# Seven block products for eight in gate, up and the queries of a transformer layer, with fp32r sums on 64-row halves and queries passed through DRAM

## The chip, the cores and the metric

One core of a Trainium2 chip. The metric is device time in microseconds (us), the median of several executions.

## The reference, cut to what matters

```python
# x [2048, 448]; wq [448, 16*256]; wo [16*256, 448]; w_gate, w_up [448, 1792]; w_down [1792, 448]; all bf16
xn = layernorm(x)
q  = (xn @ wq)                                  # 16 heads of 256
k, v = last 512 rows of the caches, 8 heads, each for two query heads
s  = softmax(q @ k.T / 16) @ v @ wo             # attention branch
g  = silu((gelu(xn @ w_gate) * (xn @ w_up)) @ w_down)
return x + s * g
```

The four chunks of 512 tokens are numbered 0 to 3. A "head" below is one of the 64 pairs of head and chunk.

## The kernel before: the parts that matter

Every instruction is recorded by a helper and put into the engine's program with its semaphore waits, so all products of one helper carry one line number (L328). Gate, up and query products have 448 rows to contract: three times 128, and 64 that are left. They are made as products of 64 rows, two at a time on the two halves of the array, each half writing another PSUM bank; halfway through, the halves change banks:

```python
def group(units, lo, hi, start, stop, phases=(0, 1)):
    for p in phases:                                  # phase 1: the halves change banks
        ...
        for (b, w, wr, cols, reads, rreads, xts) in units:
            for k in ks:
                for u, j in ((0, ph), (1, 1 - ph)):   # u: half of the array, j: bank
                    rows = slice(R * u, R * u + R)    # R = 64
                    l = wr[rows] if k == NK else w(j, k)[rows]
                    lst.append((bank[b + j][:, lo:hi], l, xnT[rows, k, cols], ...))
            before = [last_row[b][0]] if ... last_row[b][1] != ph else []   # wait for the other half
```

Queries are made just before they are used, in groups of 8 or 12 heads between the heads of attention, and stay in SBUF. For one head, attention multiplies scores, takes the exponential on ScalarE, the normalisation on VectorE, transposes by DMA (SBUF to SBUF), and multiplies by the values two heads later:

```python
for m in range(NS):                                   # NS = 64
    if m in groups:                                   # 0, 8, 20, 32, 44, 56
        for i in range(m, groups[groups.index(m) + 1], 2):
            q_group(i, ...)                           # all products of two query heads
    s_mm(m)                                           # 8 products; Exp; tensor_scalar; two dma_t of 128 KB
    ...
    if len(late) == LAG:                              # LAG = 2
        pv(late.pop(0))                               # 8 products, wait for the transposes of head m - 2
```

The softmax here doesn't subtract the row's maximum and nothing guards it: scores larger than these inputs give would overflow.

Of the kernel before, what the change touches and what calls it, by code (L numbers as in the profile page):

```python
# [8 lines left out]
F32 = mybir.dt.float32  # L9

LN_EPS = 1e-5
P = 128
# [3 lines left out]
class Buf:  # L16
# [3 lines left out]
    __slots__ = ("lo", "hi", "writer", "readers")  # L20

    def __init__(self, lo, hi):
        self.lo, self.hi = lo, hi
        self.writer = None
        self.readers = []

# [10 lines left out]
class Plan:  # L37
# [16 lines left out]
    def buf(self, lo=0, size=0):  # L54
        b = Buf(lo, lo + size)
        self.bufs.append(b)
        return b

    def reuse(self, new):


        for b in new:
            for x in self.bufs:
                if x not in new and x.lo < b.hi and b.lo < x.hi:
                    b.readers.extend(x.readers)
                    if x.writer is not None:
                        b.readers.append(x.writer)

    def op(self, eng, fn, reads=(), writes=(), dma=False, after=()):
        o = Op(eng, fn, dma)  # L70
        raw = {b.writer: None for b in reads if b.writer is not None}
        deps = dict(raw)
        for b in writes:
            if b.writer is not None:
                deps[b.writer] = None
            deps.update((x, None) for x in b.readers)


        for d in deps:
            if d.eng == eng and not d.dma and not dma and (eng == "pe" or d not in raw):  # L80
                continue
            o.deps.append(d)
        o.deps.extend(after)
        for b in writes:
            b.writer, b.readers = o, []
        for b in reads:
            b.readers.append(o)
        self.ops.append(o)
        return o
# [75 lines left out]
def bass_recurrent_scan__sliding_block_cached__geglu_ffn__prompt_kernel(  # L165
# [32 lines left out]
    HG = 8  # L198
    NG = Hq // HG
    QS = 12  # L200

    es = ExitStack()
    with es:
# [3 lines left out]
        def place(name, shape, dt, at=None):  # L207
            size = {BF16: 2, F32: 4}[dt]
# [40 lines left out]
        kT, a, _ = place("kT", [P, Hkv, 2, W], BF16)  # L249
        b_kT = sbuf_bufs(a, 2 * W * 2, Hkv)  # L250
        va, a, _ = place("va", [P, Hkv, NJ, Dh], BF16)
        b_va = [K.buf() for g in range(Hkv)]
        wq, a, _ = place("wq", [P, NK, HD], BF16)
        wqr, a, _ = place("wqr", [P, Hq, P], BF16)
        b_wql = [[K.buf() for i in range(3)] for g in range(NG)]
# [8 lines left out]
        rw = base[0]  # L264
        wo, _, rw_end = place("wo", [P, NCO, D], BF16)
        b_wo = sbuf_bufs(rw, 8 * D * 2, NCO // 8)
        x4, a, a2 = place("x4", [P, NT, D], BF16, at=rw)
        b_x4 = sbuf_bufs(a, D * 2, NT)
        NXN = (rw_end - a2) // (DP * 2)
        xn, a, a2 = place("xn", [P, NXN, DP], BF16, at=a2)  # L270
        b_xn = [[K.buf(a + i * DP * 2, D * 2), K.buf(a + i * DP * 2 + D * 2, R * 2)] for i in range(NXN)]
        assert a2 <= rw_end

        rf = base[0]
        wgu, a, at = place("wgu", [P, 2, NK, F], BF16, at=rf)
        wgur, _, at = place("wgur", [P, F], BF16, at=at)
        b_wgu = K.buf(a, at - a)
        FBL = [0, 3, 6, 9, NF]
        b_wl = [[K.buf() for j in range(2)] for i in range(4)]
        b_wlr = [[K.buf() for j in range(2)] for i in range(3)]  # L280
        wd, a, at = place("wd", [P, NF, D], BF16, at=at)
        b_wd = K.buf(a, at - a)
        actT, a, at = place("actT", [P, 2, NF, QC], BF16, at=at)
        b_actT = [sbuf_bufs(a + i * NF * QC * 2, QC * 2, NF) for i in range(2)]
        NGL = 3
        gl, a, at = place("gl", [P, NGL, QC], BF16, at=at)
        b_gl = sbuf_bufs(a, QC * 2, NGL)


        NPT, NPN, NP32 = 3, 3, 3  # L290
        pT, a, at = place("pT", [P, NPT, 2, 2, NJ, P], BF16, at=rf)
        b_pT = [sbuf_bufs(a + i * QC * NJ * 2, QC * NJ, 2) for i in range(NPT)]
        pn, a, at = place("pn", [P, NPN, 2, W], BF16, at=at)
        b_pn = sbuf_bufs(a, 2 * W * 2, NPN)
        p32, a, at = place("p32", [P, NP32, W], F32, at=at)
        b_p32 = sbuf_bufs(a, W * 4, NP32)
        assert at <= b_wgu.hi
        oT, a, at = place("oT", [P, NCO, QC], BF16, at=b_wgu.hi)
        b_oT = sbuf_bufs(a, QC * 2, NCO)
        qT, a, at = place("qT", [P, QS, 2, QC], BF16, at=b_gl[0].lo - (QS - HG) * 2 * QC * 2)  # L300
        assert b_oT[-1].hi <= a
        b_qT = [[K.buf(a + (h * 2 + e) * QC * 2, QC * 2) for e in range(2)] for h in range(QS)]

# [7 lines left out]
        def qs(n):  # L311
            return QS - 1 - n % QS

# [7 lines left out]
        def act(o, i, func, reads, writes, scale=1.0):  # L321
            K.op("act", lambda e, o=o, i=i: e.activation(o, i, func, scale=scale), reads, writes)  # L322
# [167 lines left out]
        def gu_evac(n, b):  # L490
            c, f = divmod(n, NF)
            s = n % NGL
            act(gl[:, s, :], bank[b], ACT.Gelu_apprx_tanh, (b_ps[b],), (b_gl[s],))
            K.op("dve", lambda e: e.tensor_tensor(actT[:, c % 2, f, :], bank[b + 1], gl[:, s, :], ALU.mult),  # L494
                 (b_ps[b + 1], b_gl[s]), (b_actT[c % 2][f],))

        def down(c, pairs):
            for t4 in range(4):
                t = c * 4 + t4
                b = bk(pairs, t4)  # L500
                mms([(bank[b][:, 0:D], actT[:, c % 2, f, t4 * P:(t4 + 1) * P], wd[:, f, :], f == 0, f == NF - 1)
                     for f in range(NF)], [b_wd] + b_actT[c % 2], (b_ps[b],))
# [66 lines left out]
        def load_k(g):  # L569
            dma_t(kT[:, g, :, :], A_k_cache[0, g, Sk - W:Sk, :], (), (b_kT[g],))  # L570

        def load_v(g):
            dma("pool", va[:, g, :, :],
                A_v_cache[0, g, Sk - W:Sk, :].rearrange("(j p) d -> p j d", p=P), (), (b_va[g],))

        def load_wq(g):
            lo, hi = g * HG * Dh, (g + 1) * HG * Dh
            dma("pool", wq[:, :, lo:hi], A_wq[0:K3, lo:hi].rearrange("(k p) f -> p k f", p=P), (), (b_wql[g][0],))
            for e in range(2):
                dma("pool", wqr[R * e:R * e + R, g * HG:(g + 1) * HG, :],  # L580
                    A_wq[K3:D, lo:hi].rearrange("p (h e f) -> p h e f", e=2, f=P)[:, :, e, :], (), (b_wql[g][1 + e],))

        DOWN_AT = {NF + 5: 0, 2 * NF + 1: 1}
# [4 lines left out]
        NU = NQC * NF  # L588
        cur, nxt = (0, 2), (4, 6)
        for n in range(4, NU, 2):  # L590
# [4 lines left out]
            if ln_t[0] < 8 or n >= 12:  # L595
                ln_a()
            cur, nxt = nxt, cur
# [4 lines left out]
            if n == 32:  # L602
                for g in range(NG):
                    load_wq(g)
                for g in range(Hkv):
                    load_v(g)
                for g in range(Hkv):
                    load_k(g)
                K.reuse(b_wo)
                for i in range(NCO // 8):  # L610
                    dma("pool", wo[:, i * 8:(i + 1) * 8, :],
                        A_wo.rearrange("(c p) d -> p c d", p=P)[:, i * 8:(i + 1) * 8, :], (), (b_wo[i],))
                for t in range(NXR):
                    dma("pool", xr[:, t, :], x_view[:, t, :], (), (b_xr[t],))
            if n + 1 in DOWN_AT:
                down(DOWN_AT[n + 1], cur)
                cur, nxt = nxt, cur


        def q_group(n, pairs):  # L620

            c, h = divmod(n, Hq)
            units = [(b, lambda j, k, i=i: wq[:, k, (h + i) * Dh + j * P:(h + i) * Dh + (j + 1) * P],
                      wqr[:, h + i, :], slice(c * QC, (c + 1) * QC), b_wql[h // HG][:1], b_wql[h // HG][1:], b_xnT[c * 4:c * 4 + 4])
                     for i, b in enumerate(pairs)]
            group(units, 0, QC, True, True)
            for i, b in enumerate(pairs):
                s = qs(n + i)
                act(qT[:, s, 0, :], bank[b], ACT.Copy, (b_ps[b],), (b_qT[s][0],))
                K.op("dve", lambda v, s=s, b=b: v.tensor_copy(qT[:, s, 1, :], bank[b + 1]),  # L630
                     (b_ps[b + 1],), (b_qT[s][1],))
# [3 lines left out]
        def s_mm(m):  # L635
            s, g = qs(m), m % Hq // 2
            for t4 in range(4):
                b = AB[t4]
                mms([(bank[b], qT[:, s, e, t4 * P:(t4 + 1) * P], kT[:, g, e, :], e == 0, e == 1) for e in range(2)],
                    [b_kT[g]] + b_qT[s], (b_ps[b],))  # L640
# [51 lines left out]
        NS = NQC * Hq  # L692
        groups = [0, HG] + list(range(HG + QS, NS, QS)) + [NS]

        act(tmp[:, 1, 0:1], nhalf[:, :], ACT.Exp, (b_nhalf,), (b_tmp[1][0],))
        K.reuse([b for y in b_qT[QS - HG:] for b in y])
        AB.extend(bk(cur, j) for j in range(4))
        BB.extend(bk(nxt, j) for j in range(4))
        for m in range(NS):
            if m in groups:  # L700
                for i in range(m, groups[groups.index(m) + 1], 2):
                    q_group(i, (cur, nxt)[i // 2 % 2])
                if m == 0:
                    K.reuse([b for x in b_pT for b in x] + b_pn + b_p32)
            s_mm(m)
            if m < LAG:
                down(NQC - LAG + m, nxt)
                if m == LAG - 1:
# [85 lines left out]
```

## Time and profile before

556.33 us (556.25 to 556.43). How to read the table: a matrix product that runs back to back with its neighbours starts 0.216 us after them (512 columns, 128 rows, or a pair of 64-row products), so a stage's floor can be counted.

| what | number | from |
|---|---|---|
| span of the profiled run | 554.7 us | page |
| TensorE busy | 547.6 us, 99% | engine table |
| TensorE's share of the chain of waits | 98% | chain |
| one head (16 products) | 3.45 us | distance of its first Exp to that of the next |
| first score product | 126.6 us | tile of the keys |

The top of the page of the kernel before: engine, busy us, share of the span, instructions.

```profile
span 554.7 us, 9719 instructions
PE 547.6 (99%) x3603; PEld 261.2 (47%) x3628; DVE 317.2 (57%) x817; ACT 273.6 (49%) x727; POOL 32.7 (6%) x64
```

From its costliest groups (line, engine, operation, written tile <- read tiles, shapes, count, then busy us and mean ns of one, then idle time before):

```profile
L328 PE MATMUL bank<-pT,va 128*128 128x512 bf16 x512 | 120.8, 379 | 0.0
L328 PE MATMUL bank<-xnT,wq 64*128 64x512 bf16 x768 | 94.4, 376 | 0.0
L328 PEld LDWEIGHTS bank<-xnT,wq 64*128 64x128 bf16 x768 | 36.9, 94 | 46.5 <-ACT p L643 2.1
```

TensorE (PE) never idles before a query or a value product, and a weight load (PEld) of 64 rows takes 94 ns, far less than the product over which it hides.

A window of 20 us that holds only heads of attention, kernel before: the second line is start:end, length, busy time of each engine with instructions, granted clock, share of the 16 DMA engines, GB/s.

```profile
core 0: us, PE busy (x) PEld busy (x) DVE busy (x) ACT busy (x) POOL busy (x), PEclk, DMA share, GB/s
368.00:388.00 20.00, 19.89 (x92) 9.09 (x93) 16.67 (x53) 16.83 (x53) 0.00 (x0) 1.00 0.82 158
```

And the tile of the transposed probabilities, kernel before:

```profile
L319 SPq DMA_TRANSPOSE pT<-pn x128: 1231/1261/2443, 129.0 to 524.0; - x128
  DVE pn L647: 5.4, 6
  PEld bank L328: 0.2, 1
DMA to landing us min/median/max: 2.7/2.8/4.6
```

In this tile view the first line gives size and number of the transfers, the indented lines tell who waited for them (us in all, times), and the last one how long they took from issue to landing. The transposes alone fill 0.82 of the DMA engines in this window (0.71 to 0.82 in the windows of heads that were read), and they land in 2.8 us, so that TensorE practically never waits for one.

### The profile page before, as it was taken

The page shows a single profiled execution, that of the slowest core. Times are in us where ns is not written, and L with a number is a line of the kernel's source. Part 1 is how long each engine was busy: PE and PEld are TensorE (multiplying, and loading weights), DVE is VectorE, ACT ScalarE, POOL GpSimd, SP SyncE. Part 2 cuts the span into 40 slices and gives each one's busy share as a digit, 9 for nine tenths or more (in the row PEclk, how much of TensorE's full clock was granted, in tenths as well). Part 3 has the DMA queues.
Part 4 walks back from the last instruction along what each step waited for, and adds up shares of the span by engine and source line. Part 5 has one row for each costly group of instructions (what it writes and reads, how often), then busy time and mean ns, then how long its engine had stood idle before and what let it go on. Part 6 is the DMA issues. An engine that isn't in the chain of part 4 may idle for free.

```text
span 554.7 us, 9719 instructions
## 1 busy us (share of the span) xinstructions
PE 547.6 (99%) x3603; PEld 261.2 (47%) x3628; DVE 317.2 (57%) x817; ACT 273.6 (49%) x727; POOL 32.7 (6%) x64
## 2 busy tenths in 40 slices
PE   8999999999999999999999999999999999999997
PEld 5554444444544444554444444544444454444455
DVE  6673734443385588326588745258747625858722
ACT  5432324353485588205588635058747505758600
POOL 1120580000000000000000000000000000000000
PEclk9999999999999999999999999999999999999999
DMA  9540399901156077413086803157704713618601
GB/s 295 115 141 9 79 302 307 213 1 39 38 134 96 5 149 157 88 35 92 1 153 152 153 1 77 33 94 164 146 11 95 134 34 90 153 19 153 153 8 34
DMA packets 163599, 57.63 MB, mean 104 GB/s; under 512 B 151456, under 2 KB 160672, under 8 KB 163552
## 3 DMA queue, kind: packets, MB, share of 16 engines
q1 hardware_dynamic: 159488, 45.16, 38.8%
q0 software_dynamic: 3296, 11.27, 6.7%
q8 instruction: 29, 0.48, 0.4%
q10 hardware_dynamic: 768, 0.57, 0.3%
q14 instruction: 18, 0.15, 0.1%
HBM read 17.92 MB, written 1.84 MB: 36 GB/s over the span
## 4 chain that ended last, share of the span: by engine, by line
PE 98%; DMA 1%; issue 0%; DVE 0%; SPq 0%; ACT 0%
PE bank L328 98%; DMA x<-in_A_x_dram 1%; SPq L316 0%; DVE stats L375 0%; ACT xnT L322 0%; DVE tmp L681 0%; ACT ve L391 0%; DVE ofin L684 0%; PE bank L426 0%; DVE mv L378 0%
## 5 line engine op out<-in xcount | busy, mean ns | idle before, releaser
L643 ACT ACTIVATE p<-bank 128x512 f32<-128x512 f32 x256 | 149.2, 597 | 103.3 <-PE bank L328 101.4
L647 DVE TENSOR_SCALAR pn<-p,rden 128x512 bf16<-128x512 f32 x256 | 124.6, 487 | 14.4 <-DMA pT<-pn 5.4
L328 PE MATMUL bank<-pT,va 128*128 128x512 bf16 x512 | 120.8, 379 | 0.0
L328 PE MATMUL bank<-kT,qT 128*128 128x512 bf16 x487 | 117.8, 379 | 2.0 <-ACT qT L322 1.0
L328 PE MATMUL bank<-wo,oT 128*128 128x448 bf16 (+2 forms) x544 | 97.7, 341 | 0.0
L328 PE MATMUL bank<-xnT,wq 64*128 64x512 bf16 x768 | 94.4, 376 | 0.0
L328 PE MATMUL bank<-xnT,wgu 64*128 64x512 bf16 (+2 forms) x768 | 83.9, 350 | 0.4 <-ACT xnT L322 0.4
L328 PEld LDWEIGHTS bank<-pT,va 128*128 128x128 bf16 x512 | 50.1, 98 | 60.4 <-DMA pT<-pn 0.2
L328 PEld LDWEIGHTS bank<-kT,qT 128*128 128x128 bf16 x512 | 49.6, 98 | 61.3 <-issue 2.5
L328 PEld LDWEIGHTS bank<-wo,oT 128*128 128x128 bf16 x544 | 52.0, 98 | 45.5
L630 DVE CAST qT<-bank 128x512 bf16<-128x512 f32 x64 | 42.9, 692 | 51.9 <-PE bank L328 51.9
L322 ACT ACTIVATE qT<-bank 128x512 bf16<-128x512 f32 x64 | 38.2, 597 | 60.7 <-PE bank L328 59.1
L328 PEld LDWEIGHTS bank<-xnT,wq 64*128 64x128 bf16 x768 | 36.9, 94 | 46.5 <-ACT p L643 2.1
L322 ACT ACTIVATE gl<-bank 128x512 bf16<-128x512 f32 x56 | 33.2, 597 | 49.4 <-PE bank L328 46.2
L494 DVE TENSOR_TENSOR actT<-bank,gl 128x512 bf16<-128x512 f32 x56 | 37.8, 689 | 33.4 <-PE bank L328 26.6
L328 PEld LDWEIGHTS bank<-xnT,wgu 64*128 64x128 bf16 x768 | 36.9, 94 | 37.4 <-issue 0.7
L643 ACT ACTIVATION_READ_ACCUMULATOR p<-bank 128x1 f32 x256 | 52.8, 206 | 0.0
L646 DVE RECIPROCAL rden<-rsum 128x1 f32<-128x1 f32 x256 | 40.4, 158 | 20.6 <-ACT p L643 20.0
L681 DVE SCALAR_TENSOR_TENSOR tmp<-bank,g 128x448 f32<-128x448 f32 (+2 forms) x17 | 10.1, 597 | 72.5 <-PE bank L328 72.5
L666 DVE CAST oT<-bank 128x512 bf16<-128x512 f32 x64 | 43.8, 684 | 6.9 <-PE bank L328 6.9
L328 PE MATMUL bank<-wd,actT 128*128 128x448 bf16 x224 | 43.0, 353 | 0.0
L322 ACT ACTIVATE oT<-bank 128x512 bf16<-128x512 f32 x64 | 39.1, 611 | 7.0 <-PE bank L328 7.0
(39 smaller groups left out, 182.9 us busy)
## 6 DMA issues: line engine op xcount, KB each, us to landing
wo<-in_A_wo_dram POOLq DMA_DIRECT2D x4, 896.0 KB, 19.0
wq<-in_A_wq_dram POOLq DMA_DIRECT2D x2, 1536.0 KB, 10.0
va<-in_A_v_cache_dram POOLq DMA_DIRECT2D x8, 256.0 KB, 13.9
pT<-pn SPq DMA_TRANSPOSE x128, 2.8
xr<-in_A_x_dram POOLq DMA_DIRECT2D x16, 112.0 KB, 2.3
out_dram<-ofin SPq DMA_DIRECT2D x15, 112.0 KB, 1.7
wd<-in_B_w_down_dram SPq DMA_DIRECT2D x1, 1568.0 KB, 7.6
x<-in_A_x_dram SPq DMA_DIRECT2D x2, 448.0 KB, 4.4
```

What stands on the lines that cost most here:

```text
L322: K.op("act", lambda e, o=o, i=i: e.activation(o, i, func, scale=scale), reads, writes)
L328: ins = e.matmul(o, lhsT=l, rhs=r, start=st, stop=sp)
L494: K.op("dve", lambda e: e.tensor_tensor(actT[:, c % 2, f, :], bank[b + 1], gl[:, s, :], ALU.mult), (b_ps[b + 1], b_gl[s]), (b_actT[c % 2][ ...
L630: K.op("dve", lambda v, s=s, b=b: v.tensor_copy(qT[:, s, 1, :], bank[b + 1]), (b_ps[b + 1],), (b_qT[s][1],))
L643: K.op("act", lambda e, b=b, r=r, z=z: e.activation(p32[:, z, :], bank[b], ACT.Exp, scale=att_scale, accum_out=rsum[:, r:r + 1]), (b_ps[b] ...
L646: K.op("dve", lambda e, r=r: e.reciprocal(rden[:, r:r + 1], rsum[:, r:r + 1]), (b_rsum[r],), (b_rden[r],))
L647: K.op("dve", lambda e, r=r, z=z, y=y, t=t4 % 2: e.tensor_scalar(pn[:, y, t, :], p32[:, z, :], rden[:, r:r + 1], None, op0=ALU.mult), (b_p ...
L666: K.op("dve", lambda v, i=i, b=b: v.tensor_copy(oT[:, i, :], bank[b]), (b_ps[b],), (b_oT[i],))
L681: K.op("dve", lambda e: e.scalar_tensor_tensor(out=tmp[:, s, c0:c1], in0=bank[b][:, c0:c1], scalar=0.5, in1=g2[:, t, c0:c1], op0=ALU.mult, ...
```

## The change

The intent: take one slot in fourteen of TensorE away. For two chunks of tokens and two weight blocks (gate and up; or the two 128-column halves of a query head), the 256 x 256 part of the contraction is a 2 x 2 block product. Seven products of sums give it in place of eight (Winograd's form), so 26 products of 64 rows stand for 28. This is done for 46 blocks: 14 of gate and up in chunks 2 and 3, 32 of the queries. The sums are kept in fp32r, a 4-byte type that the TensorE multiplies. Every product is split into two 64-row halves, laid into 13 slots per block by a table of offsets made by hand or search, and a small scheduler that models the engines gives the order. Because a query product now covers two chunks at once, all queries are made ahead of attention, stored to DRAM (64 times 256 KB), and loaded back, 8 heads ahead.

```diff
+        xf1, b_xf1, o = rhs_forms(57 * KB, "xf1")        # sums of activations, F32R
+        wf, a, at = at_(o, "wf", [P, NWF, 7, 2, P], F32R) # sums of weights, made on GpSimd
+        qd = nc.dram_tensor("q_all", [NQC * Hq, P, 2 * QC], BF16)
...
+        GP = 13
+        AT = {'P1l': 2, 'P1h': 0, 'P2l': 9, 'P2h': 11, 'L11a': 7, ..., 'Lda': 39, 'Ldb': 40, 'Ldh': 35}
+        SLOT, PSEM, ESEM = 0.216, 0.40, 0.03      # the scheduler's costs: PSEM + ESEM from half to half
...
+            p1 = mm(at("P1l", "P1h"), A, LH, Wb(B1, 0), X(0, t1), rb(r1), ready, **wt)        # bf16
+            seed = copy_task(..., lambda: bk_(C), lambda: bk_(A), ...)                         # bank to bank, ScalarE
+            p6 = mm(at("P6l", "P6h"), C, LH, Wf(1), Xf(1), rf(1, 1), fd(1, 1, seed), extra=ws) # fp32r
+            p5 = mm(at("P5l", "P5h"), C, LH, Wf(0), Xf(0), rf(0, 0), fd(0, 0, sU), extra=ws)   # fp32r
...
         for m in range(NS):
-            if m in groups:
-                for i in range(m, groups[groups.index(m) + 1], 2):
-                    q_group(i, (cur, nxt)[i // 2 % 2])
             s_mm(m)
+            load_q("pool", m + QS)                 # QS = 8
```

(Cut: buffers, the scheduler, copies and sums that put the results together, the loads of weights, K and V, which moved to another queue.) The names P1 to P7 are the seven products, L11 to L22 and Ld those of the rows left over; l and h are the halves of the array. P3 to P7 and Ld are fp32r: 598 of the 1196 half products.

## The prediction

> **What bounds it now.** TensorE. The engine table gives PE 547.6 us busy of 554.7, the chain of waits is 98% PE, and PE waited for other engines for under 3 us in all (waits view). Starts in the timeline are 0.216 us apart per 128x512 product (16 products per head, 3.45 us) and per pair of 64-row products (gate and up of two tiles, 28 halves, 3.02 us). Counting columns: gate/up 84.6, queries 96.7, scores 110.6, values 110.6, output 96.9, down 42.4, sum 541.8 us; the rest is the first 10 us and the tail.
>
> **What the change removes.** One of 14 slots in 46 blocks (14 of gate/up, 32 of queries): 46 x 0.216 = 9.9 us. The six switches into query groups (0.16 us of issue each) go too, about 1 us. So the best case is about 545.4 us, 2.0% faster.
>
> **What it adds.** Beside PE, per block of 13 slots (2.8 us): one ScalarE copy that seeds a bank (0.6), two more copies (0.6 or 0.69), two VectorE adds (0.69), and on GpSimd weight sums and, for gate/up, a product (an estimate of about 3 us per block, partly made beforehand). VectorE then needs about 2.7 of the 2.8; it fits, barely. If fp32r products run at the bf16 rate, PE stays the bound there. Half of the 598 slots in blocks are fp32r, so 33 ns more per slot would eat the gain. The Trainium skill (TensorE: Matmul & The Clock Gate, Weight-path perf modes) says that fast weight load is not used for FP32; no trace here has such loads yet. Bf16 loads show 94 ns; I expect longer ones to stay hidden. The skill (TensorEngine Tiling, Gotcha 1) says that row tiles must not access one PSUM bank at once: PE waits for its own earlier half (379 ns a product) at each change of half; the offsets should mostly hide this.
>
> **DMA is the second cost.** Queries write and read 16.8 MB. The queue table gives about 303 GB/s at full share for copies and about 197 GB/s for transposes (worked out): 55 us of all engines for the stores, 55 for the loads. Query stage: stores, weights, K and V make about 88 us of DMA in about 97. Attention: windows now show a DMA share of 0.71 to 0.79, or 2.66 of 3.45 us per head; a 256 KB query load adds 0.87, so 3.5 of 3.45: saturated in the stretches of 16 heads, relieved in the output products (12 us each). At its start wo (3.7 MB, 12 us of DMA) collides with the transposes. The two-head lag absorbs part; I expect 2 to 6 us of PE waits here, and 1 to 3 us in the block stages.
>
> **Sum.** 556.3 - 10.9 + 5 = about 550.5 us, range 545.5 to 559. Faster by over 2%: 5%; within 2%: 87%; slower by over 2%: 8%.
>
> **What would show it.** Right: block stages at about 2.8 us per block with PE above 95% busy; fp32r products starting as densely as bf16; DMA share above 0.9 in attention, transposes landing later than the 2.8 us of now, and PE or VectorE waiting for them, mostly among the first heads. Wrong: fp32r starts over 0.25 us apart per pair, PE waiting for GpSimd or VectorE in the blocks (too little engine time), or a DMA share near 1 without any PE wait (gain nearer 10 us).
>
> **What would make it wrong.** Slow fp32r weight loads (then 560 or more), or DMA that overlaps better or worse than shares add.

## The result, and the profile after

The kernel after took 597.34 us (593.69 to 601.29, 4 runs) against 556.38 (556.25 to 556.56, 4 runs): slower, ratio 1.0736, 95% interval 1.0675 to 1.0797. The profiled run was the fastest of the four.

The top of the page, kernel after:

```profile
span 591.6 us, 10358 instructions
PE 569.8 (96%) x3592; PEld 306.0 (52%) x3592; DVE 365.2 (62%) x890; ACT 318.8 (54%) x806; POOL 147.2 (25%) x243
```

Groups of the kernel after: the fp32r products and their weight loads (xf, wf are the sums), bf16 query products of the same blocks, and the value products.

```profile
L706 PE MATMUL bank<-xf,wf 64*128 64x512 f32 x598 | 158.2, 443 | 0.7 <-POOL xf L625 0.7
L378 PE MATMUL bank<-pT,va 128*128 128x512 bf16 x512 | 121.0, 379 | 14.9 <-DMA pT<-pn 14.9
L706 PEld LDWEIGHTS bank<-xf,wf 64*128 64x128 f32 x598 | 100.7, 185 | 43.6 <-PE bank L706 35.1
L706 PE MATMUL bank<-xnT,wq 64*128 64x512 bf16 x320 | 93.1, 382 | 2.1 <-ACT bank L372 2.0
```

Two new things stand there. An fp32r weight load takes 185 ns where a bf16 one took 94, and 35.1 us of the idle time before these loads end with a product of TensorE itself. The value products, which waited for nothing before, wait 14.9 us for transposes.

Windows of the kernel after: the whole block stage, then two windows of heads only.

```profile
60.90:242.00 181.10, 178.16 (x1366) 118.47 (x1363) 115.74 (x176) 100.88 (x179) 82.52 (x122) 1.00 0.50 149
346.00:366.00 20.00, 19.16 (x90) 8.53 (x89) 14.81 (x49) 15.92 (x49) 3.04 (x6) 1.00 1.10 210
366.00:386.00 20.00, 19.41 (x91) 8.65 (x90) 16.09 (x51) 16.43 (x51) 3.50 (x6) 1.00 1.06 217
```

The tile of the transposed probabilities, kernel after:

```profile
L369 SPq DMA_TRANSPOSE pT<-pn x128: 1231/1241/6189, 246.6 to 562.0; - x128
  DVE pn L1171: 42.9, 44
  PEld bank L378: 23.8, 19
  PE bank L378: 14.9, 16
DMA to landing us min/median/max: 2.7/3.9/12.0
```

The share of the DMA engines went from between 0.71 and 0.82 to 1.06 and above, the median landing from 2.8 to 3.9 us and the longest from 4.6 to 12.0. The Trainium skill (DMA: Bandwidth & Descriptors, Issuing engines are not separate DMA queues) says that transfers issued by different engines end up on the same 16 DMA engines and interleave; this trace agrees, since loads issued by GpSimd delayed transposes issued by SyncE.

The span splits into three stages:

| stage, us | after | floor | lost |
|---|---|---|---|
| start, chunks 0 and 1 | 60.9 | 60.9 | 0 |
| blocks, to the first score product | 181.4 (to 242.3) | 150.3 (46 blocks of 13 slots of 0.216; 21.1 for the down products of two chunks) | about 31 |
| attention, to the end | 349.3 | 331.6 (measured below, without reloads) | 17.7 |

The floors add to 542.8 us, 11.9 below the span of before, where the prediction had counted 10.9 (the first floor is simply this kernel's own time, so the table shows no loss there). The count of saved slots was right to about 1 us. Everything else was lost in two places. Note that the block stage shows PE busy in 178.2 of 181.1 us while it lost some 31. The Trainium skill (Perfetto Trace Analysis, Tensor Engine Instruction (MATMUL, LD_WEIGHTS)) says that the end of a product in the profile is estimated, not observed; so busy time of a pipelined engine does not measure its rate. Starts do: the copies that seed a bank (one per block) stand 3.32 us apart (median; 3.31 in the recorded texts) where 13 slots of 0.216 make 2.81. Over 46 blocks these 0.51 us make 23 of the 31 us; the other 8 lie in single longer blocks, which were not taken apart in this kernel.

How this comes about shows in the weight loads of the kernel after, a stretch of one block (start, us, engine, operation, count, idle before and what ended it):

```profile
95.25 0.18 PEld L706 LDWEIGHTS bank<-xf,wf 64*128 64x128 f32 x1 [0.25 <-PE bank L706]
95.28 0.17 PEld L706 LDWEIGHTS bank<-xnT,wgu 64*128 64x128 bf16 x2
95.36 0.19 PEld L706 LDWEIGHTS bank<-xf,wf 64*128 64x128 f32 x1
95.84 0.18 PEld L706 LDWEIGHTS bank<-xf,wf 64*128 64x128 f32 x1 [0.29 <-PE bank L706]
```

When a product follows one that the other half of the array made in the same bank, it waits for that product. The wait stands ahead of its weight load in the program, so the load (0.18 us) begins only at 95.25 or 95.84, when the wait ends, and neither it nor the product has anything to hide behind.

All 1364 products of the block stage were matched to the plan, by their ends. By the plan nine products per block wait like this. Three are costly: P6l came 0.454 us after its predecessor on its half of the array, P5h 0.455, P7h 0.354 (medians, from end to end). The other six came within 0.216 to 0.248, so for them the offsets did hide the wait. L11a came 0.351 us after its predecessor; it waits for no product, but stands right behind P7h in the program. An fp32r product that merely follows another came after 0.231 to 0.236, where the plan had 0.216 for nearly all. In one half of the array this adds to the period: 0.24 (P5h) + 0.14 (P7h) + 0.13 over the other products (0.02 to 0.03 at each of seven) makes 0.51 over 2.81. In the other half it is 0.24 (P6l) + 0.14 (L11a) and again 0.13. So about three quarters of the lost 0.51 us come with the costly changes of half; the rest, about 6 us in 46 blocks, is spread over products most of which do not wait. Slow helper engines are not the main cause: in this profile the products of the blocks waited 2.0 us for ScalarE and 0.7 for GpSimd in all, their weight loads 4.6 and 1.0.

### The profile page after: what moved, and what is told of

The parts are those of the page before. It is cut to its first block, busy times and chain, and to the rows that moved or that the text cites. A ratio compares the mean times of both kernels' runs of the same rounds, so it can differ in the third digit from the quotient of the medians.

```text
span 591.6 us, 10358 instructions
## 1 busy us (share of the span) xinstructions
PE 569.8 (96%) x3592; PEld 306.0 (52%) x3592; DVE 365.2 (62%) x890; ACT 318.8 (54%) x806; POOL 147.2 (25%) x243
## 4 chain that ended last, share of the span: by engine, by line
PE 75%; DMA 17%; DVE 4%; POOL 2%; ACT 1%; issue 1%; DVEq 0%; ACTq 0%; POOLq 0%
PE bank L378 49%; PE bank L706 25%; DMA pT<-pn 15%; DVE pn L1171 2%; DMA q_all<-qo 1%; PE bank L495 1%; POOL xf L625 1%; POOL wf L625 1%; ACT bank L372 0%; DVE oT L1190 0%; DVE qo L732 0%; ACT qo L372 0%; DVE rden L1170 0%; POOL xf L628 0%; ACT gl L372 0%
## 5 line engine op out<-in xcount | busy, mean ns | idle before, releaser
L706 PE MATMUL bank<-xf,wf 64*128 64x512 f32 x598 | 158.2, 443 | 0.7 <-POOL xf L625 0.7
L1171 DVE TENSOR_SCALAR pn<-p,rden 128x512 bf16<-128x512 f32 x256 | 124.7, 487 | 50.6 <-DMA pT<-pn 42.9
L378 PE MATMUL bank<-pT,va 128*128 128x512 bf16 x512 | 121.0, 379 | 14.9 <-DMA pT<-pn 14.9
L706 PEld LDWEIGHTS bank<-xf,wf 64*128 64x128 f32 x598 | 100.7, 185 | 43.6 <-PE bank L706 35.1
L378 PE MATMUL bank<-kT,qT 128*128 128x512 bf16 x512 | 121.0, 379 | 0.0
L706 PE MATMUL bank<-xnT,wq 64*128 64x512 bf16 x320 | 93.1, 382 | 2.1 <-ACT bank L372 2.0
L378 PEld LDWEIGHTS bank<-pT,va 128*128 128x128 bf16 x512 | 48.6, 98 | 79.7 <-DMA pT<-pn 23.8
L366 POOL DMA_DIRECT2D qT<-q_all x60 | 34.1, 569 | 202.5 <-PE bank L378 173.6
L378 PE MATMUL bank<-xnT,wgu 64*128 64x512 bf16 (+2 forms) x432 | 43.0, 331 | 0.1
L706 PE MATMUL bank<-xnT,wgu 64*128 64x512 bf16 x140 | 41.7, 382 | 0.0
L366 POOL DMA_DIRECT2D xr<-in_A_x_dram x16 | 8.6, 539 | 121.4 <-DVE ofin L1208 104.8
L706 PE MATMUL bank<-xnT,wqr 64*128 64x512 bf16 x96 | 36.1, 376 | 0.0
```

The lines of the kernel that those rows point to most:

```text
L366: K.op(q, lambda e, o=o, i=i: e.dma_start(o, i), reads, writes, dma=True)
L378: ins = e.matmul(o, lhsT=l, rhs=r, start=st, stop=sp)
L706: o = K.op("pe", lambda e: e.matmul(bank[bi][:, 0:w_], lhsT=l, rhs=r, start=st, stop=True, skip_group_check=True), reads(), (b_ps[bi],), a ...
L1171: K.op("dve", lambda e, r=r, z=z, y=y, t=t4 % 2: e.tensor_scalar(pn[:, y, t, :], p32[:, z, :], rden[:, r:r + 1], None, op0=ALU.mult), (b_p ...
```

## The experiments

All kernels returned outputs within the tolerance. Some have wrong queries; the tolerance doesn't see that, because the attention branch is a small part of the output. The letters in the expectations: W says that fp32r weight loads and the waits at changes of half cost the block stage its time; D that the reloads of queries saturate the DMA engines in attention. Other letters are rivals, explained where they occur.

### a_bf16: the sums in bf16

```diff
-        t, a, at = at_(off, name, [P, 7, QC], F32R)
+        t, a, at = at_(off, name, [P, 7, QC], BF16)      # same addresses, half the bytes
-        wf, a, at = at_(o, "wf", [P, NWF, 7, 2, P], F32R)
+        wf, a, at = at_(o, "wf", [P, NWF, 7, 2, P], BF16)
```

> The changed kernel with the sums of weights and of inputs kept in bf16 in place of fp32r (same addresses, same order of instructions). Theory W (a block lasts 3.31 us and not 2.81 mainly because a product that waits for the other half's product in its bank starts its fp32r weight load, 183 ns, only then): blocks fall to 2.85 to 3.05 us, the time to 572 to 585 us. Rival L (the wait from half to half is longer than the layout allows, whatever the type): blocks stay at 3.2 or more, time over 588 us. The result may be less exact.

Measured: 586.96 us (585.72 to 592.76), ratio 1.0574 (1.0522 to 1.0626), a little over the expected time. The block stage took 168.0 us instead of 181.4, its period 2.98 us instead of 3.32, which is inside what W expected of the blocks and refutes rival L. The time fell by only 10.4 us, because attention took 356.2 us in this profile instead of 349.3. The groups of the sums' products and loads, this kernel:

```profile
L707 PE MATMUL bank<-xf,wf 64*128 64x512 bf16 x598 | 140.4, 378 | 0.7 <-POOL xf L626 0.7
L707 PEld LDWEIGHTS bank<-xf,wf 64*128 64x128 bf16 x598 | 50.5, 93 | 53.7 <-PE bank L707 23.4 <-issue 1.5 <-POOL xf L626 1.0
```

The load is 93 ns again, and the product after a change of half follows in 0.228 (P6l) and 0.245 (P5h) instead of 0.454 and 0.455. So W holds for 13 us. This is the type's whole effect, at the waits and between them. The weight loads still waited 23.4 us for TensorE itself: the plan reckons 0.43 us from half to half, which is all but two slots (0.432), so that any longer wait moves a block. The rest of the block stage's loss, about 18 us, stays with bf16 sums too.

### a_noload: no reload of queries after the first eight heads (wrong queries on purpose)

```diff
             s_mm(m)
-            load_q("pool", m + QS)
```

> The changed kernel, but queries are loaded back from DRAM for the first 8 heads only and used again for the others (wrong result on purpose). Theory D (DMA capacity: a 256 KB query load per head beside the transposes makes 768 KB per head): the attention stage falls from 350 to about 335 us, every head at 3.45 us, time 578 to 583 us. Rival G (the stretches of 16 heads without query products between leave ACT, VectorE and transposes no pause): time stays over 590 us.

Measured: 575.23 us (574.24 to 575.53), ratio 1.0344 (1.0327 to 1.0362). Attention took 331.6 us instead of 349.3, and nearly every head 3.45. A window of heads only, this kernel:

```profile
345.00:365.00 20.00, 20.00 (x95) 9.08 (x93) 16.67 (x53) 17.14 (x54) 0.00 (x0) 1.00 0.78 158
```

The DMA share is back at 0.78 and PE's gaps are gone. D holds, and it is worth more than expected.

### b_store: the kernel before, with a store of 256 KB per head

```diff
-            s_mm(m)
+            o = s_mm(m)
+            K.op("pool", lambda e, m=m: e.dma_start(junk[m % 4], kT[:, m % Hkv, :, :]...), ..., dma=True, after=[o])
```

> The kernel before, with one more DMA of 256 KB per head in the attention (a store of K from SBUF to an unused DRAM buffer, issued by GpSimd after the head's scores): right result. Theory D: heads of the stretches slow from 3.45 to 3.7 or more, time 563 to 575 us. Rival G: time stays under 559 us.

Measured: 560.51 us (559.25 to 560.99), ratio 1.0074 (1.0059 to 1.0089): +4.4 us; in the profiles attention took 432.3 us for 428.1. The DMA share rose to 1.04 in one window of heads and was 0.84 to 1.09 in others. Neither expectation was met: the mechanism works in the kernel before too, but weakly. Two reasons are open here: query products stand between stretches of 8 or 12 heads, in which the DMA engines could catch up, and a store is not a load. This run cannot tell them apart; a_store does.

### a_bf16_noload: both

> Both edits together (wrong result on purpose). If the two losses are independent, the gains add within 3 us: 556 to 568 us by theories W and D; what then still lies above 545 us is left to other causes.

```diff
-        t, a, at = at_(off, name, [P, 7, QC], F32R)
+        t, a, at = at_(off, name, [P, 7, QC], BF16)      # and wf likewise
-            load_q("pool", m + QS)
```

Measured: 564.04 us (562.15 to 564.64), ratio 1.0136 (1.0118 to 1.0154). From 1.0736, bf16 alone takes 0.016 and no loads alone 0.039; both together 0.060, where the sum is 0.055. The two gains add up to within 0.005, or 3 us. What is left, 7.9 us over before, is neither of them. It lies in the blocks, 169.0 us for a floor of 150.3 (attention took 332.9 us): the changes of half that remain and, as argued below, the stores of queries.

### a_half: loads of 128 KB instead of 256 (wrong queries on purpose)

```diff
-                dma(q, qT[:, qs(m), :, :].rearrange("p e q -> p (e q)"), qd[m], ...)
+                if m < QS: ...                                  # as before
+                else: dma(q, qT[:, qs(m), 0, :], qd[m][:, 0:QC], ...)
```

> The changed kernel, but each query load after the eighth head brings only the first half of the head's query (128 KB, wrong result on purpose). Attention lost 17.7 us with full loads and nothing with none. Theory D (capacity, a threshold): 2.66 us of transposes and about 0.75 us of load fit in 3.45 us a head, so nearly all of the loss goes: 574 to 580 us. Rival P (each load delays the transposes beside it in proportion to its bytes, threshold or not): half of the loss stays, 582 to 588 us.

Measured: 579.78 us (578.05 to 580.27), ratio 1.0416 (1.0395 to 1.0436). The loss in attention is 5.3 us (336.9 instead of 331.6), not half of 17.7. A window of heads, this kernel:

```profile
346.00:366.00 20.00, 19.95 (x93) 8.88 (x92) 16.84 (x53) 16.73 (x53) 3.56 (x6) 1.00 0.93 186
```

Half the bytes cost under a third of the loss, as D expected. So the loss is not proportional to the bytes; it rises steeply when the share comes near 1. That it begins at one threshold is not shown: only two sizes were run, in another window of this run (366 to 386 us) the share was 1.01 and PE busy 19.29 of 20 us, and a share also rises when packets get slow, so it is in part an effect.

### a_store: a store of 256 KB per head in place of the load (wrong queries on purpose)

```diff
-            load_q("pool", m + QS)
+            K.op("pool", lambda e, m=m: e.dma_start(junk[m % 4], kT[:, m % Hkv, :, :]...), ..., dma=True, after=[o])
```

> The changed kernel without query loads after the eighth head, but with a 256 KB store of K per head to an unused DRAM buffer in their place (wrong result on purpose, the same store that cost the kernel before only 4.4 us). Theory S (stores burden the transposes less than loads do, whatever the kernel): 577 to 583 us. Rival K (any 256 KB per head costs the changed kernel's longer stretches about 18 us): 590 us or more.

Measured: 581.49 us (580.39 to 581.93), ratio 1.0449 (1.0434 to 1.0465), with 5.3 us lost in attention. A window of heads, this kernel:

```profile
346.00:366.00 20.00, 19.50 (x90) 8.53 (x89) 16.38 (x52) 16.79 (x54) 3.41 (x6) 1.00 1.01 219
```

The same bytes cost a third as much as stores (theory S: a store is cheaper than a load beside transposes). And since the store cost about as much here as in b_store (5.3 and 4.4 us), the query products between the heads of the kernel before were not the main reason that it was cheap there. I read the packets of attention: 4 KB packets of the loads took about 250 ns on average (244 to 305 by window; median 159), those of the stores about 188 (median 160); the transposes' packets took 21 to 23 ns in both, 20 without either. So loads have a tail of slow packets. Why, no run shows; it stays open.

### a_batch_bf16: bf16, and the reloads of 16 heads at once during the output products

The output products (24 us once in 16 heads) need no transposes. Reloading there needs 21 query buffers instead of 8, which half-size sums make room for.

```diff
-    QS = 8
+    QS = 21
-            load_q("pool", m + QS)
+            if m in (2, 6, 10): load_wo("pool", ..., [o])       # wo spread over the first heads
...
-                        wo_mm(0, BB[0], 0, NCO - 2)
+                        o = wo_mm(0, BB[0], 0, NCO - 2)
+                        for i in range(m + 1, m + 1 + Hq): load_q("pool", i, [o])
```

> A mended version: bf16 sums, 21 query slots, the loads of the next 16 heads issued together when the output products of a chunk start (no transposes then), ten heads loaded during the block stage, K, V and part of wo loaded more spread out, three more buffers for query stores. If the loads hurt only because they meet the transposes, attention is within 3 us of the 331.6 us that it took without loads; blocks 160 to 167 us; time 555 to 563 us. If loads cost as much wherever they stand: over 570 us.

Measured: 573.34 us (569.73 to 575.82), ratio 1.0301 (1.0259 to 1.0342), so over the expected 555 to 563 and, by the number alone, in the rival's range (loads cost as much wherever they stand). The profile speaks against the rival: the second, third and fourth stretches of 16 heads ran clean at 3.45 us a head, with all queries loaded. The first stretch did not: heads of 5.3, 5.4, 4.3 and 6.3 us stand beside the 896 KB loads of wo, and one block took 7.6 us where early loads of queries were issued ahead of stores on the same queue. Attention took 339.8 us, 8 over its floor, and the blocks 166.9.

### a_batch_at: the same, with a searched table of offsets

```diff
-  AT = {... 'P2l': 9, 'L11a': 7, 'L11b': 8, 'P6h': 8, 'P5h': 18, 'P3h': 28, 'L12b': 30, 'P7h': 20, ...}
+  AT = {... 'P2l': 7, 'L11a': 8, 'L11b': 9, 'P6h': 7, 'P5h': 19, 'P3h': 29, 'L12b': 27, 'P7h': 22, ...}
```

(Twelve offsets move. The search was given the measured half-to-half distances instead of 0.43 us.)

> As the one before, with the order of the products in a block searched anew for a wait from half to half of 0.475 us and not 0.43 (as the traces show it for bf16): blocks 2 to 5 us less than in the one before, time 551 to 560 us. If the residue of blocks comes from query stores and the start instead: no difference over 1 us.

Measured: 575.47 us (573.08 to 578.95), ratio 1.0349 (1.0307 to 1.0391): no faster than the one before, so the expectation failed, though the period fell from 2.98 to 2.92 us as meant. In the profile (mean clock 0.99) a single head took 12.5 us beside a load of wo, whose transpose landed after 10.6 us and during which the granted clock fell to 0.55 to 0.60; one block took 8.3 us. So the loads of wo could still do harm. Three windows of this kernel show the stall and the clock after it (the column before the DMA share):

```profile
264.00:268.00 4.00, 0.00 (x0) 0.00 (x0) 1.37 (x5) 1.28 (x4) 0.00 (x0) 1.00 0.79 132
268.00:272.00 4.00, 1.35 (x4) 0.53 (x5) 1.23 (x5) 0.69 (x2) 0.00 (x0) 0.60 1.06 220
272.00:276.00 4.00, 4.00 (x12) 1.45 (x11) 1.77 (x5) 1.39 (x4) 0.00 (x0) 0.55 0.58 131
```

The kept traces of the other runs show the same order. TensorE stood still for 1.8 us or more only in a_bf16, a_batch_bf16, a_batch_at, a_best and a_fp_at, eleven times in all; after seven of these stalls the granted clock fell to 0.50 within 2 to 5 us of the stall's start. The other profiles have no such stall and no such fall before their very end. So one late transfer cost more here than its own wait. No run was made to test this, so it is an association in these traces and not a shown cause.

### a_best: wo in pieces of 224 KB, early loads after the stores

```diff
-                load_wo("pool", (0, 2, 3)[m // 4], [o])         # 896 KB
+            if 4 <= m < 12: load_wo("pool", m // 4 + 1, m % 4, [o])   # 224 KB; half of wo earlier, among the blocks
-    QS = 21;  QE = 10;  9 store buffers
+    QS = 17;  QE = 9;   6 store buffers
```

> A second mended version: bf16 sums and the searched order of products; V and half of wo loaded while gate and up run (no DMA traffic there), K spread over the query stage, nine heads' queries loaded early one by one, the rest of wo in eight pieces of 224 KB, one a head, and the queries of the next 16 heads in one batch when the output products of a chunk start. If what was left in the first mended version came from loads that landed in bursts (one stall of 4 us in the blocks, 9 in the first stretch): blocks 158 to 162 us, attention 332 to 336 us, time 553 to 559 us, within 1% of the kernel before. If bursts were not the cause: over 565 us.

Measured: 563.35 us (562.91 to 564.22), ratio 1.0128 (1.0113 to 1.0143): better by 12 us, yet over the expected 553 to 559. Attention took 333.8 us, near its 331.6 and as expected. The block stage did not improve (167.8 us, where 158 to 162 was expected); copies of queries now waited for store buffers. Who waited for the tile in DRAM, this kernel:

```profile
L372 SPq DMA_DIRECT2D q_all<-qo x64: 319/320/582, 121.6 to 226.6; - x64
  ACT qo L378: 4.9, 5
```

### a_fp_at: fp32r kept, only the offsets searched

> The changed kernel with fp32r sums as they were, only the order of the 26 products of a block searched anew for a wait from half to half of 0.63 us and not 0.43. Theory W (weights exposed behind waits that the layout was drawn too tightly for): blocks 3.31 us fall to 3.0 to 3.2, time 583 to 592 us. Rival F (fp32r products and loads are slow in themselves, in whatever order): blocks stay within 0.05 us of 3.31, time as the changed kernel's, 593 us or more.

```diff
-  AT = {... 'L11a': 7, 'L11b': 8, 'P5h': 18, 'P3h': 28, 'P7h': 20, 'L22b': 14, 'P4l': 37, 'Ldb': 40, 'Ldh': 35}
+  AT = {... 'L11a': 8, 'L11b': 7, 'P5h': 19, 'P3h': 30, 'P7h': 14, 'L22b': 22, 'P4l': 39, 'Ldb': 37, 'Ldh': 31}   # and four more
```

Measured: 594.13 us (590.56 to 595.1), ratio 1.0661 (1.0623 to 1.0699), over the time that W expected and by that number in rival F's range. The period decides against F: it fell from 3.32 to 3.11 us, inside W's 3.0 to 3.2, and the first score product came at 234.7 instead of 242.3 us. The time did not follow because attention took 358.1 us in this profile for 349.3 (one head of 11.1 us). The group of the weight loads, this kernel:

```profile
L706 PEld LDWEIGHTS bank<-xf,wf 64*128 64x128 f32 x598 | 89.0, 186 | 11.9 <-DVE qo L732 2.3 <-issue 1.5 <-POOL xf L625 1.0
```

The loads are as long as before (186 ns), but no wait for TensorE is left among what ended their idle time (35.1 us before), and the period is still 0.31 over the plan's 2.81. By this, of 0.51 us per block, 0.20 belonged to offsets too tight for these loads. Of the 0.31 left, 0.11 also stays with bf16 sums and searched offsets (2.92 us, a_batch_at), so 0.20 is left to the type and the longer distances it asks for.

### a_best_qo: five more store buffers

```diff
+        qo2, a, _ = at_(102 * KB, "qo2", [P, 5, 2, QC], BF16)   # 11 for 6
-        QE = 9
+        QE = 5
```

> a_best with five more buffers for the outgoing queries (11 for 6; the price is that 5 for 9 of the query loads are issued before attention begins) and nothing else. In a_best the stores of queries held up copies (bank seeds 3.8 to 5.0 us apart instead of 2.92, the chain of waits gives a store 2.7% of the span). If waiting for a free store buffer is what is left over in the block stage (theory Q), first score product falls from 228.7 us to about 221 to 225 and the time to 555 to 561. If the buffers don't matter (DMA is full either way, or the blocks' 2.92 us period holds all of it), the time stays within 562 to 565.

Measured: 558.08 us (557.46 to 558.89), ratio 1.0029 (1.0012 to 1.0045), as theory Q said; the first score product came at 222.0 us instead of 228.7. The same tile, this kernel:

```profile
L374 SPq DMA_DIRECT2D q_all<-qo x64: 319/320/1490, 121.6 to 219.9; - x64
  ACT qo L380: 0.8, 1
```

The wait for buffers fell from 4.9 to 0.8 us, and the block stage by 6.7. One thing more changed, though: QE went from 9 to 5, so four fewer early loads of queries were issued on SyncE's queue, which also issues the stores (in a_best a load stood ahead of waiting stores there at 186 to 188 us, for instance). The 6.7 us belong to both changes together; no run separates the buffers from the loads.

### a_best2: the same with a more careful model in the scheduler

```diff
-        SLOT, PSEM, ESEM = 0.216, 0.40, 0.03
+        SLOT, PSEM, ESEM = 0.216, 0.445, 0.03                  # and stores of 4 us for 2.5, loads of 5 for 3
```

> The same with a layout made for what the traces show: the planner reckons with 0.445 us between the halves of one bank instead of 0.40, a store of queries with 4 us instead of 2.5, and the loads that SyncE issues with 5 us. By theory Q with a better order: 553 to 560 us, about the time of before. If the layout's reckoning doesn't matter, as a_best_qo.

Measured: 558.25 us (557.88 to 558.54), ratio 1.0035 (1.002 to 1.005): as a_best_qo. These numbers of the model made no difference here.

No version beats the kernel before; the best is 0.3% behind it and 6.6% ahead of the kernel after. Against the best case (542.8), a_best_qo's span of 557.1 us has 10.8 us left in the block stage (161.1 for 150.3) and 3.5 in attention (335.1 for 331.6). Of the 10.8, about 5 are 46 blocks at 2.92 instead of 2.81 us; the remainder is spread over single longer blocks and was not taken apart.

## Why the prediction was wrong, point by point

- Right: what bounded the kernel before, and what could be saved. The floors of the three stages add to 542.8 us against a span of 554.7, so 11.9 us could be saved; the prediction had 10.9.
- Wrong, and the largest step: "Bf16 loads show 94 ns; I expect longer ones to stay hidden", with "1 to 3 us in the block stages". Measured: about 31 us, of which the type accounts for the 13.4 that bf16 sums took back; the rest is the changes of half in either type (next point) and single longer blocks. The loads took 185 ns, and they stayed hidden only where no late wait stood ahead of them. At the costly changes of half (P6l, P5h) the load began only when the wait ended, and the product came after 0.454 us instead of 0.228 or 0.245 with bf16 sums. The prediction held both facts (no fast weight load for FP32 by the Trainium skill, TensorE: Matmul & The Clock Gate, Weight-path perf modes, which the 185 ns against 94 agree with; and the wait at a change of half), but treated them as two separate costs. They meet at the same place: the wait takes away the very product behind which the load would hide. Its own warning, that 33 ns more per fp32r slot would eat the gain, was to the point: 0.51 us per block is 78 ns for each of its 6.5 fp32r slots, though it arises at a few of them.
- Wrong: "the offsets should mostly hide this". The offsets assume 0.43 us from half to half for both types, with a margin of 2 ns against two slots. They hid the wait at six of nine changes, not at P6l, P5h and P7h. With bf16 sums the period was still 2.98 us, and searched offsets brought it to 2.92; with fp32r sums they brought it from 3.32 to 3.11.
- Right in mechanism: "saturated in the stretches of 16 heads", share above 0.9 (1.06 to 1.10), later transposes (3.9 us), and PE and VectorE waiting for them (14.9 and 42.9 us). Wrong in size: "2 to 6 us of PE waits" were 17.7 us lost. The mis-sized term is the 0.87 us that a query load adds, worked out from what copies took by themselves. The prediction added 0.87 to 2.66 and got 3.5 of 3.45 us, over by 0.05 per head. Measured, the share was 0.78 without loads and 1.06 to 1.10 with them, so that a load added 0.28 to 0.32 of 3.45 us, or 1.0 to 1.1 us; a store added 0.8 (0.78 to 1.01). Why a load takes more beside transposes stays open, and the share alone does not give the loss: at 1.01 it was 5.3 us with stores.
- Wrong: only "mostly among the first heads". The stalls came in every stretch until the last load: the heads of the four stretches took about 6.0, 5.7, 4.7 and 1.5 us more than 3.45 us each would.
- Left out: stores of queries holding up the copies. More buffers for them, with fewer early loads on their queue, were worth 6.7 us of block stage in the bf16 version (a_best against a_best_qo).

## What to carry to other kernels

Where products of two row halves take turns in one bank, ask for each wait whether the weight load stands behind it, and what that load costs in the type used; a type whose products follow each other almost as fast (0.23 us here for 0.216) can lose much more at the waits (0.45). A steady DMA stream beside the transposes cost 5.3 us here at a share of about 0.93 and 17.7 at 1.06 to 1.10; move it in bulk to a stage that needs no transposes, in pieces. Check an engine's rate by starts per period, not by its busy share.

## What the Trainium skill lacked or had wrong

- TensorE: Matmul & The Clock Gate, LDWEIGHTS: P/1.2 gives 107 ns for 128 columns and names no type. The runs show 93 to 98 ns for bf16 and 185 to 186 ns for fp32r; the page's section on weight-path modes says that FP32 gets no fast load, without a figure.
- The same page, Back-to-back issue gap: it says that N/2.4 + 2.5 (216 ns at 512 columns) over-counts for a stream of loads and products, which would sustain 131 ns. In these runs 16 products with their loads took 3.45 us, 216 ns each, in hundreds of heads; nothing came near 131. For fp32r, for which it has no figure, products that follow one another stood 231 to 236 ns apart.
- The same page, Step-by-step, says that weight loads are pulled ahead of products in flight, and not what a semaphore wait does to that. Here the load started only when the wait ended: 0.454 us from product to product with fp32r sums at P6l, 0.228 with bf16.
- TensorEngine Tiling (Array Packing), Gotcha 1, says that row tiles may not access one bank at once, and gives no price for taking turns. At the costliest turns here it was 0.24 us over the plain 0.216 in fp32r and up to 0.05 in bf16, with products placed 0.43 us apart by the plan.
- No page that I found says what loads, stores and DMA transposes cost each other: about 250 ns on average for a 4 KB packet of a load beside transposes, 188 for one of a store, and 17.7 against 5.3 us lost by TensorE for the same bytes.
